# A fused attention and feed-forward kernel on one core: one written order for all five engines up to step 17, some of GpSimd's operations on VectorE, and other places for the turned queries

## The chip, the core and the metric

The kernel runs on one core of a Trainium2 chip. The core has five engines with a line of instructions each, which are taken strictly one after the other: TensorE (PE in the profile, its weight loads PEld), VectorE (DVE), ScalarE (ACT), GpSimd (POOL) and SyncE (SP), which here issues every DMA. The metric is the device time in microseconds of one execution, lower is better.

## What is computed

Per batch (8) and head (8), with 576 positions and 64 columns, queries are normalised over the columns, keys over the positions, and no attention matrix is formed. The result, laid out as 4608 tokens by 512, goes through a feed-forward block.

```python
q_s = exp(q - max(q, -1)); q_s /= sum(q_s, -1) + 1e-9
k_s = exp(k - max(k, 2));  k_s /= sum(k_s, 2) + 1e-9
kv  = einsum('bhsd,bhse->bhde', k_s, v)
x   = einsum('bhsd,bhde->bhse', q_s, kv)   # -> 4608 x 512
h   = x @ w_in                             # w_in 512 x 2048, float64
out = (h - tanh(h)) @ w_out                # w_out 2048 x 512, float64
```

## The kernel before

**Numbers.** The products are made of two float32r parts each (a rounded part and the rest), three matmuls for one: high by high, high by rest, rest by high. So every operand needs a cast (ScalarE) and a subtraction (the rest). The weights come as the two 32-bit words of a float64 and are decoded on the chip, one piece of 128 x 512 at a time, 16 pieces `i` of w_in and 16 pieces `o` of w_out: a clamp on VectorE (L118), two scalings on ScalarE (L121, L124), a shift-and-or on VectorE (L127), the cast on ScalarE (L133) and the rest on GpSimd (L134).

**Steps.** Tokens are taken in nine chunks of 512, the 2048 hidden columns in 16 pieces; a step is one pair (chunk, piece), 144 in all. The steps go 0,0 to 0,7, then all 16 of chunk 1, then 0,8 to 0,15, then chunk after chunk, so that step n is (0,n) for n below 8 and (1,n-8) for n from 8 to 23. A step has 12 matmuls `ph` (L484), then on ScalarE `u`, `t`, `vv`, `m` (L488 to L496) and the cast `gh` (L501), on VectorE `g` (L492), `t` minus (L497), `g` again (L498) and a predicated copy (L499), on GpSimd the rest `gl` (L504), and 12 matmuls `po` (L527), which PE takes two steps later. Chunk 0's first half is laid aside in DRAM (`aside`) and added later.

**Attention.** A batch needs the maximum of its keys `km` (L193 to L197), its transposition `pm` and spreading `pb`, a subtraction and exp of the keys, 40 small matmuls `pk` (L265), and the division into `kvs` (L278 to L281). Queries are reduced and subtracted (`mq` L341, GpSimd L342), exp'd, summed (`sq` L355), multiplied on GpSimd (`qn` L380), turned on PE (`pt` L395), copied (`qs` L400), multiplied with `kvs` (`px` L421), and split into `xh` (L434) and `xl` (L435), the input of `ph`. Chunk 0 needs batch 0, chunk 1 batch 1 and so on.

**What sets the order.** A first block (L591 to L645) fixes all five engines by the order of the code: batch 0, pieces i0 and i1, and the first chunk's queries. After that only PE and SP follow the code (L661); where VectorE, ScalarE and GpSimd take the steps, the decoding and batch 1's preparation is decided by a scheduler with its own idea of durations, when the program is built. Decoding is handed out at a rate of `FIRST, THEN, SPREAD` (L568), over steps 0 to 19. Batch 1's loads, all of them, stand in SP's line ahead of the pieces i4, o3 and later (`gate`, L87); the pieces i11, o10 and later stand behind the four `aside` stores.

**Places.** Pools hand out tile places by tag. `qs`, `qn` and `km` share three places (tag `qs`). `spare_q` lies in chunk 1's `xl` place, one v tile in the place of w_i15, one q tile in that of w_o15; both are late weights.

## Time and profile before

| what | value |
|---|---|
| median of 3 runs | 929.22 us (928.27 to 931.55) |
| the profiled execution | 932.16 us |
| its span, first to last instruction | 930.0 us |
| busy over the span: PE, PEld, DVE, ACT, POOL | 96%, 78%, 66%, 55%, 36% |
| first `ph` matmul of step 0 | 32.23 us |
| first `ph` matmul of step 18 (1,10) | 169.84 us |

The profile is of one execution; positions are in us from the span's start. A row of a group gives line, engine, operation, out<-in, shape and count, then after the bar its busy time, the mean ns of one, and the idle time of the engine just before with what ended it. A row of windows gives busy time (and instructions) of each engine within a stretch, then the clock granted to PE as a share and the DMA's share and rate. A row of waits gives who waited <- for what, the us in total, the times, the longest. A row of the chain gives start, length and what.

### The profile page before, as it was taken

What the parts mean: (1) busy time and instruction counts of PE and PEld (TensorE: products, weight loads), DVE (VectorE), ACT (ScalarE), POOL (GpSimd) and SP (SyncE); (2) the same over time, 40 slices, a digit from 0 to 9 for tenths busy, and PEclk for the clock granted to TensorE, in tenths of its full rate; (3) what the DMA queues carried; (4) which work ended last, traced back from release to release, by engine and by line L of the source; (5) the groups of instructions that cost most, each with busy time, mean ns of one, the idle gap of its engine ahead of it and who ended that gap; (6) DMA issues with size and microseconds to landing.
All of it is one profiled execution on the core that took longest, in us unless ns stands there. A gap on an engine that the chain in (4) does not pass through costs nothing.

```text
span 930.0 us, 13178 instructions
## 1 busy us (share of the span) xinstructions
PE 890.6 (96%) x4996; PEld 723.6 (78%) x4996; DVE 610.6 (66%) x875; ACT 555.0 (60%) x967; POOL 333.3 (36%) x277
## 2 busy tenths in 40 slices
...
GB/s 269 297 202 2 1 289 96 1 42 118 1 114 40 119 2 46 35 103 24 24 45 102 24 1 68 76 39 1 88 28 0 1 69 12 1 1 46 1 1 45
DMA packets 79775, 57.47 MB, mean 62 GB/s; under 512 B 14688, under 2 KB 72032, under 8 KB 79712
## 3 DMA queue, kind: packets, MB, share of 16 engines
...
## 4 chain that ended last, share of the span: by engine, by line
PE 75%; DVE 9%; DMA 6%; ACT 6%; issue 2%; POOL 2%; SPq 0%; DVEq 0%; ACTq 0%; POOLq 0%
PE po L527 35%; PE ph L484 34%; DMA q<-in_q_dram 3%; PE pk L265 2%; DVE g L498 2%; DMA k<-in_k_dram 2%; PE px L421 1%; PE pt L395 1%; DVE g L499 1%; DVE g L492 1%; DVE t L497 1%; ACT gh L501 1%; ACT t L490 1%; ACT u L488 1%; DMA raw_i<-in_moe_w_in_dram 1%
## 5 line engine op out<-in xcount | busy, mean ns | idle before, releaser
L527 PE MATMUL po<-w_o,gh 128*128 128x512 f32 x1152 | 361.6, 395 | 0.5 <-ACT gh L501 0.5
L504 POOL TENSOR_TENSOR gl<-g,gh 128x512 fp32r<-128x512 f32 x143 | 193.0, 1350 | 416.7 <-ACT gh L501 389.9
L484 PE MATMUL ph<-xh,w_i 128*128 128x512 f32 x1152 | 317.9, 398 | 5.0 <-ACT xh L434 3.5
L484 PEld LDWEIGHTS ph<-xh,w_i 128*128 128x128 f32 x1152 | 214.8, 190 | 52.5 <-ACT xh L434 5.0
L527 PEld LDWEIGHTS po<-w_o,gh 128*128 128x128 f32 x1152 | 215.9, 189 | 48.4 <-issue 1.4
L492 DVE SCALAR_TENSOR_TENSOR g<-u,ph 128x512 f32<-128x512 f32 x144 | 98.3, 683 | 227.6 <-ACT t L490 225.7
L527 PE MATMUL po<-w_o,gl 128*128 128x512 f32 x576 | 226.9, 394 | 9.4 <-POOL gl L504 9.4
L501 ACT CAST gh<-g 128x512 fp32r<-128x512 f32 x144 | 89.4, 621 | 193.0 <-DVE g L499 188.5
L484 PE MATMUL ph<-xl,w_i 128*128 128x512 f32 x576 | 156.3, 393 | 2.2 <-DVE xl L435 2.2
L498 DVE SCALAR_TENSOR_TENSOR g<-vv,g 128x512 f32<-128x512 f32 x144 | 124.6, 865 | 22.4 <-ACT vv L494 11.9
L527 PEld LDWEIGHTS po<-w_o,gl 128*128 128x128 f32 x576 | 109.0, 189 | 34.9 <-POOL gl L504 11.1
L488 ACT ACTIVATE u<-ph 128x512 f32<-128x512 f32 x144 | 85.8, 596 | 76.1 <-PE ph L484 75.9
L484 PEld LDWEIGHTS ph<-xl,w_i 128*128 128x128 f32 x576 | 108.5, 189 | 27.4 <-DVE xl L435 3.8
L499 DVE COPY_PREDICATED g<-m,t 128x512 f32<-128x512 int32 x144 | 120.1, 834 | 3.7
L496 ACT ACTIVATE m<-ph 128x512 int32<-128x512 f32 x144 | 86.5, 601 | 35.5 <-DVE g L492 35.2
L494 ACT ACTIVATE vv<-u,b_pa 128x512 f32<-128x512 f32 x144 | 104.8, 727 | 1.7 <-DVE g L498 1.7
L497 DVE TENSOR_TENSOR t<-ph,t 128x512 f32<-128x512 f32 x144 | 97.8, 679 | 1.9 <-ACT m L496 1.8
L490 ACT ACTIVATE t<-ph 128x512 f32<-128x512 f32 x144 | 85.3, 593 | 0.0
L342 POOL TENSOR_TENSOR q<-q,mq 128x1024 f32<-128x1024 f32 x15 | 30.1, 2009 | 61.8 <-DVE mq L341 57.0
L380 POOL TENSOR_TENSOR qn<-q,sq 128x512 f32<-128x512 f32 x30 | 32.4, 1082 | 24.2 <-PE pt L395 13.0
L341 DVE TENSOR_REDUCE mq<-q 128x16 f32<-128x1024 f32 x15 | 18.3, 1218 | 25.7 <-DMA q<-in_q_dram 25.7
L134 POOL TENSOR_TENSOR w_o<-c_o,w_o 128x512 fp32r<-128x512 f32 x16 | 25.7, 1605 | 8.4 <-ACT w_o L133 8.3
...
## 6 DMA issues: line engine op xcount, KB each, us to landing
...
out_dram<-o SPq DMA_DIRECT2D x28, 256.0 KB, 2.1
...
```

Source lines behind the costliest of these rows:

```text
L484: nc.tensor.matmul(ph, w[:, i, c], x[:, c, :], start=(n == 0), stop=(n == len(ops) - 1))
L488: nc.scalar.activation(u, ph, AF.Square)
L490: nc.scalar.activation(t, ph, AF.Tanh)
L492: nc.vector.scalar_tensor_tensor(g, u, C2, ph, op0=ALU.mult, op1=ALU.mult)
L494: nc.scalar.activation(vv, u, AF.Square, bias=b_pa)
L496: last = nc.scalar.activation(m, ph, AF.Square, scale=M_SCALE)
L497: nc.vector.tensor_tensor(t, ph, t, op=ALU.subtract)
L498: nc.vector.scalar_tensor_tensor(g, vv, PB, g, op0=ALU.add, op1=ALU.mult)
L499: nc.vector.copy_predicated(g, m, t)
L501: nc.scalar.copy(gh, g)
L504: eng.tensor_tensor(gl, g, gh.bitcast(F32), op=ALU.subtract)
L527: nc.tensor.matmul(po[t], g[:, cols], wt["o", f][:, w], start=(begin and n == 0), stop=(end and n == 2),)
```

## The change

A string `ORDER` of 576 names lists every small operation of the first 17 steps (n from 0 to 16, their `po` up to step 14), of batches 0 and 1, of chunk 0's and 1's first 512 tokens' queries, of the loads and of the decoding of all 32 pieces. Each operation that was a part of a longer function has become a function of its own, and the list calls them one by one, inside a block that fixes all five engines. Two lines of it:

```python
u0 st.i4 k1.2 t0 ld.i6 vv0 g0 m0 tt0 ca.i4 gg0 ph2 v1.0 u1 sub.i4 t1 g1 vv1 tt1 lo.o2 ld.i7 gg1
pr.o2 cp0 u2 st.o2 pr.o1 k1.1 cl.i6 gh0 st.o1 m1 gl0* t2 ph3 q3 cp1 ca.o2 ca.o1 cl.i5 sub.o2*
```

`ld` is a load, `cl pr lo st ca sub` the decoding, `u t vv m g tt gg cp gh gl` a step. A star puts an operation on VectorE that else is GpSimd's: 31 names have one, 15 `sub`, 13 `gl`, 2 `qn` and 1 `qu` (the query subtraction). From step 17 on the code is as before, but no piece is left to decode; the scheduler still places the other three engines' instructions of later steps, and some of batch 2 come among the listed ones. The core of the diff:

```diff
-        with tc.issue_after(gate[-1].ins) if gate else nullcontext():
-            ...
-            nc.gpsimd.tensor_tensor(w[:, 1], cf, w[:, 0].bitcast(F32), op=ALU.subtract)
+        def rest(eng):
+            w = wt[kind, f]
+            eng.tensor_tensor(
+                w[:, 1], st["c"].bitcast(F32), w[:, 0].bitcast(F32), op=ALU.subtract
+            )
+        return dict(cl=clamp, pr=scale, lo=low, st=shift, ca=cast, sub=rest)
...
+    def q_keep(i: int):
+        unit, j = tiles[i]
+        late = {(0, 0): f"wo{NF - 3}", (1, 0): f"wo{NF - 2}", (1, 1): f"wi{NF - 2}"}
+        if unit in late and unit not in spare:
+            spare[unit] = wts.tile([P, 2, NC, P], F32, name=f"spare_qs{i}", tag=late[unit])
+        if unit in spare:
+            qs = spare[unit][:, j]
+        else:
+            qs = ap.tile([P, NC, P], F32, name=f"qs{i}", tag="qs", bufs=3)
+        nc.scalar.copy(qs, qs_of[i])
...
+        def gl(eng):
+            eng.tensor_tensor(
+                new("gl", F32R), st["g"], st["gh"].bitcast(F32), op=ALU.subtract
+            )
...
-    FIRST, THEN, SPREAD = 4, 2 * F0 + 1, 12
+    PLANNED, SPREAD = 17, 3
...
     with tc.manual_schedule(engines={ENG.PE, ENG.DVE, ENG.Activation, ENG.Pool, ENG.SP}):
-        kv_load(0, st)
-        ...
+        for name in ORDER.split():
+            eng = (nc.vector,) if name[-1] == "*" else ()
+            ...
+            ops[name](*eng)
+            done.add(name)
...
-        for n, (j, f) in enumerate(steps):
+        for n, (j, f) in enumerate(steps[PLANNED:], PLANNED):
```

The turned queries of the tiles (0,0), (1,0) and (1,1) so lie in the places of w_o13, w_o14 and w_i14 until `px` has read them; those three pieces can be loaded only after that.

**PE, from step 0 on.** `ph0_1` is `ph` of chunk 0, piece 1; `po0_0_2` is the sum of chunk 0 that was opened at piece 0, token tile 2, and the `w_o` beside it tells the piece; the last number of a name is the tile's own. Before:

```order
L220 MATMUL pb1_507<-ident_r_84,ml1_454 128x128
L265 MATMUL pk1_522<-v1_0_428,k1_0_422 64x65 x16
L484 MATMUL ph0_2_539<-xh0_285,w_i2_367 128x512 x4
L484 MATMUL ph0_2_539<-xl0_286,w_i2_367 128x512 x4
L484 MATMUL ph0_2_539<-xh0_285,w_i2_367 128x512 x4
L527 MATMUL po0_0_0_587<-w_o0_357,gh0_0_398 128x512 x2
L527 MATMUL po0_0_0_587<-w_o0_357,gl0_0_400 128x512
L527 MATMUL po0_0_1_591<-w_o0_357,gh0_0_398 128x512 x2
```

Now:

```order
L544 MATMUL ph0_1_433<-xh0_365,w_i1_373 128x512 x4
L544 MATMUL ph0_1_433<-xl0_366,w_i1_373 128x512 x4
L544 MATMUL ph0_1_433<-xh0_365,w_i1_373 128x512 x4
L544 MATMUL ph0_2_467<-xh0_365,w_i2_391 128x512 x4
L544 MATMUL ph0_2_467<-xl0_366,w_i2_391 128x512 x4
L544 MATMUL ph0_2_467<-xh0_365,w_i2_391 128x512 x4
L544 MATMUL ph0_3_517<-xh0_365,w_i3_429 128x512 x4
L544 MATMUL ph0_3_517<-xl0_366,w_i3_429 128x512 x4
L544 MATMUL ph0_3_517<-xh0_365,w_i3_429 128x512 x4
L635 MATMUL po0_0_0_550<-w_o0_423,gh0_0_507 128x512 x2
L635 MATMUL po0_0_0_550<-w_o0_423,gl0_0_513 128x512
```

Before, batch 1's `pm`, `pb` and `pk` stand among the first steps, with `ph` of step 2 and `po` of step 0 behind them. Now four `ph` stand in a row ahead of `po` of step 0, and batch 1's `pm` comes after `po` of step 3. Not shown: at the end of the list `ph` of step 17 now stands ahead of `po` of step 14, before it stood behind.

**VectorE, around the split of chunk 0's second half** (`xl0<-px2`). Before:

```order
L435 TENSOR_TENSOR xl0_286<-px0_0_287,xh0_285 128x2x256
L435 TENSOR_TENSOR xl0_286<-px0_1_288,xh0_285 128x2x256
L193 TENSOR_TENSOR km1_434<-k1_0_422 128x512
L127 SCALAR_TENSOR_TENSOR c_i1_266<-raw_i1_124 128x512
L196 TENSOR_TENSOR km1_434<-km1_434,k1_1_424 128x512 x2
L197 TENSOR_TENSOR km1_434<-km1_434,kr1_426 64x512
L435 TENSOR_TENSOR xl0_286<-px2_0_329,xh0_285 128x2x256
L435 TENSOR_TENSOR xl0_286<-px2_1_330,xh0_285 128x2x256
L118 TENSOR_SCALAR raw_o0_126<-raw_o0_126 128x512
L118 TENSOR_SCALAR raw_i2_128<-raw_i2_128 128x512
L341 TENSOR_REDUCE mq1_0_579<-q1_0_442 128x16
```

Now the same split, and then the first place where batch 1's `km` comes:

```order
L145 TENSOR_SCALAR raw_o2_275<-raw_o2_275 128x512
L486 TENSOR_TENSOR xl0_366<-px2_1_321,xh0_365 128x2x256
L486 TENSOR_TENSOR xl0_366<-px2_0_320,xh0_365 128x2x256
L167 TENSOR_TENSOR w_i1_373<-c_i1_363,w_i1_373 128x512
L486 TENSOR_TENSOR xl0_366<-px0_1_346,xh0_365 128x2x256
L486 TENSOR_TENSOR xl0_366<-px0_0_345,xh0_365 128x2x256
```

```order
L565 SCALAR_TENSOR_TENSOR g0_2_542<-u0_2_499,ph0_2_467 128x512
L570 TENSOR_TENSOR t0_2_515<-ph0_2_467,t0_2_515 128x512
L584 TENSOR_TENSOR gl0_1_568<-g0_1_488,gh0_1_539 128x512
L223 TENSOR_TENSOR km1_575<-k1_0_414 128x512
L573 SCALAR_TENSOR_TENSOR g0_2_542<-vv0_2_570,g0_2_542 128x512
L226 TENSOR_TENSOR km1_575<-km1_575,k1_1_504 128x512
L578 COPY_PREDICATED g0_2_542<-mk0_2_548,t0_2_515 128x512
```

Before, four operations on batch 1's keys stand ahead of the second pair of `xl`, and the reduction of batch 1's queries soon behind. Now the pairs of `xl` stand together with a `sub` of piece i1 (w_i) between them, and batch 1's `km` stands behind steps 0 and 1, with step 1's `gl`, formerly GpSimd's, just ahead of it.

**SP and VectorE, where chunk 0's first half is laid aside and batch 2 begins.** SP before:

```order
L89 DMA raw_i10_1053<-in_moe_w_in_dram 128x4x128
L94 DMA raw_o9_1105<-in_moe_w_out_dram 128x512
L551 DMA aside_100<-aside0_1118 128x512 x2
L551 DMA aside_100<-aside2_1129 128x512 x2
L89 DMA raw_i11_1167<-in_moe_w_in_dram 128x4x128
L94 DMA raw_o10_1223<-in_moe_w_out_dram 128x512
L89 DMA raw_i12_1275<-in_moe_w_in_dram 128x4x128
```

SP now:

```order
L123 DMA raw_i15_945<-in_moe_w_in_dram 128x4x128
L123 DMA raw_i14_1034<-in_moe_w_in_dram 128x4x128
L128 DMA raw_o14_1077<-in_moe_w_out_dram 128x512
L733 DMA aside_100<-aside1_1110 128x512
L733 DMA aside_100<-aside3_1152 128x512 x2
L189 DMA k2_0_1700<-in_k_dram 128x8x128
L733 DMA aside_100<-aside1_1110 128x512
L189 DMA k2_1_1702<-in_k_dram 128x8x128
L194 DMA kr2_1704<-in_k_dram 64x8x64
```

VectorE now:

```order
L584 TENSOR_TENSOR gl1_0_1183<-g1_0_1147,gh1_0_1178 128x512
L156 SCALAR_TENSOR_TENSOR c_o8_1188<-raw_o8_696 128x512
L565 SCALAR_TENSOR_TENSOR g1_1_1196<-u1_1_1185,ph1_1_1128 128x512
L570 TENSOR_TENSOR t1_2_1194<-ph1_2_1160,t1_2_1194 128x512
L573 SCALAR_TENSOR_TENSOR g1_1_1196<-vv1_1_1198,g1_1_1196 128x512
L223 TENSOR_TENSOR km2_1742<-k2_0_1700 128x512
L565 SCALAR_TENSOR_TENSOR g1_2_1223<-u1_2_1205,ph1_2_1160 128x512
L578 COPY_PREDICATED g1_1_1196<-mk1_1_1181,t1_1_1173 128x512
```

The loads of the late pieces no longer stand behind the `aside` stores; batch 2's first key tile stands behind three of them and the second behind the fourth (both take the places of the `aside` tiles). On VectorE the scheduler has set the first operation on batch 2's keys between those of steps 9 and 10.

More of the change, by code (lines that the diff above doesn't have):

```diff
@@ L1 @@
-from contextlib import ExitStack, contextmanager, nullcontext
+from contextlib import ExitStack
 import numpy as np
@@ L80, in attn_moe_kernel @@
     staged = {}
-    gate = []
     wt = {}
@@ L506, in h_step @@
+    def h_step(j: int, f: int):
+        parts = h_parts(j, f)
+        last = None
+        eng = nc.vector if (j, f) == (NCH - 1, NF - 1) else nc.gpsimd
+        for name, part in parts.items():
+            if name == "last":
+                last = part()
+            elif name == "gl":
+                part(eng)
+            else:
+                part()
         return last
@@ new lines, in o_mm @@
+        if begin:
+            po[t] = ps_o.tile([P, DM], F32, name=f"po{j}_{f}_{t}", tag="o")
+        cols = slice(t * P, (t + 1) * P)
+        for n, (g, w) in enumerate(((gh, 0), (gh, 1), (gl, 0))):
+            nc.tensor.matmul(
+                po[t],
+                g[:, cols],
+                wt["o", f][:, w],
+                start=(begin and n == 0),
+                stop=(end and n == 2),
+            )
+        if (j, f) == (0, F0 - 1):
+            spare["po", t] = po[t]
+        return end
@@ new lines, in o_aside, with o_out @@
+    def o_aside(t: int):
+        pair = "aside", t // 2
+        if pair not in spare:
+            spare[pair] = ap.tile([P, 2, DM], F32, name=f"aside{t}", tag="k", bufs=NKP)
+        spare["aside of", t] = o = spare[pair][:, t % 2]
+        nc.scalar.copy(o, spare["po", t])
+    def o_out(j: int, f: int, t: int):
+        if j == 0:
+            o = back[t // 2][:, t % 2]
+            nc.vector.tensor_tensor(o, po[t], o, op=ALU.add)
+        elif j == NCH - 1 and t % 2:
+            o = gp.tile([P, DM], F32, name=f"o{j}_{f}_{t}", tag="g")
+            nc.vector.tensor_copy(o, po[t])
+        else:
+            o = dec.tile([P, DM], F32, name=f"o{j}_{f}_{t}", tag="c")
+            nc.scalar.copy(o, po[t])
+        for rows, p0, p1 in rows_of(out, j * TPC + t):
+            nc.sync.dma_start(rows, o[p0:p1])
@@ new lines, in attn_moe_kernel @@
+    for kind, f in pieces:
+        ops[f"ld.{kind}{f}"] = lambda kind=kind, f=f: load_weight(kind, f)
+        for part, fn in split_weight(kind, f).items():
+            ops[f"{part}.{kind}{f}"] = fn
+    for n, (j, f) in enumerate(steps[:PLANNED]):
+        for part, fn in h_parts(j, f).items():
+            ops[f"{part}{n}"] = fn
+        for t in range(TPC):
+            ops[f"po{n}.{t}"] = lambda j=j, f=f, t=t: o_mm(j, f, t)
+    for t in range(TPC):
+        ops[f"ev.{t}"] = lambda t=t: o_aside(t)
+        ops[f"sv.{t}"] = lambda t=t: nc.sync.dma_start(aside[t], spare["aside of", t])
@@ L590, in attn_moe_kernel @@
     ENG = mybir.EngineType
+    done = set()
     with tc.manual_schedule(engines={ENG.PE, ENG.DVE, ENG.Activation, ENG.Pool, ENG.SP}):
-        kv_load(0, st)
-        q_load(q0)
-        q_load(q1)
-        load_weight(*pieces[0])
-        v_load(0, st, 0)
-        v_load(0, st, 1)
-        v_load(0, st, 2)
-        for n in range(1, 4):
-            load_weight(*pieces[n])
-        loaded = 4
-        decode = [split_weight(*pieces[n]) for n in range(2)]
-        def go(*ns):
-            for n in ns:
-                next(decode[n])
```

523 lines of the change are left out of this document (271 added, 252 removed).

## The prediction

> **What bounds the kernel now.** I read the page first, then the busy time by stages, then PE's waits, then the operations of VectorE one kind at a time, then the timeline at the places where PE stood.
>
> ```profile
> span 930.0 us, 13178 instructions
> PE 890.6 (96%) x4996; PEld 723.6 (78%) x4996; DVE 610.6 (66%) x875; ACT 555.0 (60%) x967; POOL 333.3 (36%) x277
> ```
>
> Over the whole span PE is busy 96%, which says little about its ends. The windows by stage, cut at 23.1 (the end of batch 0's division), 32.2 (first `ph`), 73.3 (`ph` of step 3), 142.8 and 169.8 (`ph` of step 18):
>
> ```profile
> 0.00:23.10 23.10, 17.37 (x156) 16.07 (x156) 15.00 (x24) 6.72 (x8) 8.50 (x22) 0.85 1.02 269
> 32.20:73.30 41.10, 25.38 (x140) 19.08 (x140) 34.09 (x51) 24.33 (x40) 22.45 (x13) 0.68 0.67 220
> 73.30:142.80 69.50, 68.57 (x361) 54.67 (x357) 52.41 (x77) 59.64 (x112) 37.22 (x30) 1.00 0.33 112
> 142.80:169.80 27.00, 21.84 (x85) 16.59 (x85) 24.21 (x32) 20.76 (x39) 17.10 (x13) 0.94 0.31 45
> 169.80:930.00 760.20, 751.56 (x4189) 612.84 (x4188) 479.04 (x685) 437.36 (x760) 245.06 (x201) 1.00 0.15 40
> ```
>
> Behind 169.8 PE idles 8.6 of 760 us at full clock: nothing can be gained there by the order of the first 17 steps, and I let that part move as a block. Between 73.3 and 142.8 PE idles 0.9. The loss lies in the second row, where PE idles 15.7 us at a clock of 0.68 while DVE is busy 34.1 of 41.1, and in the fourth, where PE idles 5.2 and DVE 2.8 of 27.0. The pace of PE when nothing holds it, from the chain:
>
> ```profile
> 167.28 2.72 PE po L527 x12
> 170.00 2.72 PE ph L484 x12
> ```
>
> The first `ph` of step 0 and of step 18 in the timeline:
>
> ```profile
> 32.23 2.08 PE L484 MATMUL ph<-xh,w_i 128*128 128x512 f32 x4 [0.83 <-ACT xh L434]
> 169.84 1.07 PE L484 MATMUL ph<-xh,w_i 128*128 128x512 f32 x4
> ```
>
> Up to `ph` of step 18 PE has 18 `ph` and 16 `po`: 34 x 2.72 = 92.5 us, and I put batch 1's small matmuls at 7.5 (an estimate: the stage 73.3 to 142.8 holds 23 groups, 62.6 of its 69.5 us, so four turnings and two `px` took about 6 with the idle time; `pm`, `pb`, `pk` come on top). That is 100; from 32.2 on it took 137.6. So 37 us is what a perfect order could bring with the first `ph` where it is. Who held PE, up to 169.8:
>
> ```profile
> PE po L527 <- POOL gl L504: 8.9, 3, 5.2
> PE pb L220 <- DVE mh L209: 6.6, 2, 5.0
> PE pk L265 <- ACT k L253: 3.1, 1, 3.1
> PE ph L484 <- DVE xl L435: 2.2, 2, 1.4
> ```
>
> Three are VectorE's line or GpSimd's `gl`; the third is an exp that itself waited for VectorE's subtraction. The timeline shows how a load holds what has nothing to do with it:
>
> ```profile
> 31.90 2.42 DVE L196 TENSOR_TENSOR km<-km,k 128x512 f32<-128x512 f32 x2 [0.86 <-DMA k<-in_k_dram]
> 34.96 1.27 DVE L435 TENSOR_TENSOR xl<-px,xh 128x512 fp32r<-128x512 f32 x2
> 39.14 1.22 DVE L341 TENSOR_REDUCE mq<-q 128x16 f32<-128x1024 f32 x1 [2.23 <-DMA q<-in_q_dram]
> ```
>
> `xl`, without which step 0 can't go on, stands behind batch 1's keys; step 0's own `g` comes after batch 1's queries. So up to step 17 the bound is VectorE: its work, its place in line, and what GpSimd does to it.
>
> **The change part by part.** I count VectorE's time up to the end of step 15's `gl`, the last thing that `po` of step 15 waits for. Before, the same content stands done at 165.2 (17 `g` to predicated copy, 27 shifts, 32 clamps):
>
> ```profile
> 0.00:165.20 165.20, 134.43 (x788) 106.97 (x789) 129.34 (x188) 113.59 (x201) 84.84 (x74) 0.87 0.56 163
> ```
>
> *What it has to do.* Groups within 0 to 165, mean ns of one behind the busy time:
>
> ```profile
> L504 POOL TENSOR_TENSOR gl<-g,gh 128x512 fp32r<-128x512 f32 x16 | 24.5, 1536 | 27.1 <-ACT gh L501 23.8 <-PE px L421 3.3
> L134 POOL TENSOR_TENSOR w_o<-c_o,w_o 128x512 fp32r<-128x512 f32 x13 | 21.8, 1676 | 8.2 <-ACT w_o L133 8.2
> L498 DVE SCALAR_TENSOR_TENSOR g<-vv,g 128x512 f32<-128x512 f32 x17 | 19.0, 1117 | 3.4 <-ACT vv L494 2.8
> L497 DVE TENSOR_TENSOR t<-ph,t 128x512 f32<-128x512 f32 x17 | 11.5, 678 | 0.1
> L118 DVE TENSOR_SCALAR raw_o<-raw_o 128x512 f32<-128x512 f32 x16 | 11.9, 741 | 0.9 <-DMA raw_o<-in_moe_w_out_dram 0.9
> L118 DVE TENSOR_SCALAR raw_i<-raw_i 128x512 f32<-128x512 f32 x16 | 10.3, 646 | 2.3 <-DMA raw_i<-in_moe_w_in_dram 2.3
> L127 DVE SCALAR_TENSOR_TENSOR c_i<-raw_i 128x512 uint32<-128x512 uint32 x14 | 10.8, 771 | 0.2
> L196 DVE TENSOR_TENSOR km<-km,k 128x512 f32<-128x512 f32 x6 | 6.7, 1124 | 2.5 <-DMA k<-in_k_dram 2.4
> ```
>
> `t` (L497), which reads `ph`, takes 0.68; the second `g` (L498), of the same shape and with both inputs in SBUF, 1.12. The clamp alone takes 0.42 and one beside GpSimd's work 1.5:
>
> ```profile
> 36.49 0.42 DVE L118 TENSOR_SCALAR raw_i<-raw_i 128x512 f32<-128x512 f32 x1
> 142.79 1.46 POOL L504 TENSOR_TENSOR gl<-g,gh 128x512 fp32r<-128x512 f32 x1
> 143.04 1.76 DVE L498 SCALAR_TENSOR_TENSOR g<-vv,g 128x512 f32<-128x512 f32 x1
> 144.73 1.51 DVE L118 TENSOR_SCALAR raw_o<-raw_o 128x512 f32<-128x512 f32 x1
> ```
>
> The stretched operations end as GpSimd's do. Taking 0.68 (clamp 0.42) as undisturbed, the stretching cost 17 x 0.44 + 16 x 0.32 + 16 x 0.23 + 27 x 0.09 + 6 x 0.45 = 21 us. So VectorE's bare work was 129.3 - 21 = 108. The stars add, up to that point, 13 `gl`, 13 `sub` and 2 `qn`, of 128 x 512, and one `qu` of twice the size. How long `gl` takes on VectorE one instruction shows (the last step's), and two `xl` in 1.27 above show that the second in a row adds 0.6:
>
> ```profile
> L504 DVE TENSOR_TENSOR gl<-g,gh 128x512 fp32r<-128x512 f32 x1 | 0.7, 692 | 0.8 <-ACT gh L501 0.8
> ```
>
> 28 x 0.6 + 1.2 = 18: bare work 126 us, of which nothing lies beside other VectorE work. GpSimd loses 26 x 1.5 + 4.5 = 44 of its 85 us, about 41 remain. Stretching goes with GpSimd's time and with the instructions exposed: 21 x 41/85 x 114/85 = 13.5 (85 exposed before: the second `g`, clamps, shifts, `km`; 29 more now). Ends: 0 and GpSimd's whole 41. I take 11, a little under the scaling, since a chain from `g` to `gl` that stays on VectorE meets GpSimd less.
>
> The Trainium skill ("SBUF — State Buffer", "Who interferes with whom") states that VectorE with two SBUF inputs and GpSimd reading SBUF exclude each other for a whole instruction, and "Perfetto Trace Analysis" ("Optimizing Scalar/DVE Operations") that moving work between the two might not help for that reason. The rows above agree on the exclusion; by that rule the 11 would be anything up to 41, which is the second rival. The rows also show the other side: 1.5 us of GpSimd's time is given for 0.6 of VectorE's.
>
> *Where it stands idle.* Before, 165.2 - 129.3 = 36 us:
>
> ```profile
> DVE g L492 <- ACT t L490: 11.9, 10, 1.9
> DVE km L193 <- DMA k<-in_k_dram: 5.0, 1, 5.0
> DVE sl L278 <- PE pk L265: 4.8, 1, 4.8
> ```
>
> The first key tile is still the first thing needed, and batch 0's `pk` still stands ahead of its division: 9.8 us stay. The 11.9 of `g` behind `t` come from one step's chain after another; the list puts other steps' and pieces' work between, I leave 2 of them (between 0 and 6). The waits for loads of batch 1 (2.4 and 2.2 in the rows above) go, since weights come first and batch 1's keys stand behind step 1. What comes in their place: the scheduler has set the first operation on batch 2's keys behind step 9's second `g`, and that tile's DMA stands behind three `aside` stores:
>
> ```profile
> 273.19 5.42 DMA k<-in_k_dram
> ```
>
> That is a key tile's landing later on, in the chain; and the stores, by the table of DMA issues, with the median us to landing last:
>
> ```profile
> aside<-aside SPq DMA_DIRECT2D x4, 256.0 KB, 2.1
> ```
>
> From the copy that frees the last of them: 2.1 to be stored, about 0.5 to be issued, 5.4 to land, 8 in all, against some 4 us of VectorE's work in between. That is 4 us of standing, and behind it queue step 10's `g` and all else; the second key tile, behind the fourth store, some 3 more. I take 6 (0 to 8). Idle: 9.8 + 2 + 6 = 18.
>
> *The sum.* 126 + 11 + 18 = 155 for the end of step 15's `gl`; `po` of step 15 takes 2.7 more, so `ph` of step 18 begins at 157.5 to 158 instead of 169.84. The gain is 12 us. PE's floor, 29 + 100 = 129 (first `ph` some 3 us earlier, as `xl` no longer waits for `km`), and ScalarE's, 114 of work before and no more now, both lie under it. The other edits come to nothing: splitting functions adds no instruction; eleven of the warming matmuls now stand right ahead of step 0, 2 to 4 us by the row below (two records for one, 28 before), where PE waits about 3 us for `xh` and `xl` anyhow; the queries in w_o13's place are read by batch 0's `px`, those in the places of w_i14 and w_o14 by batch 1's, and these two are the last weights that SP loads, for steps 21 and 22; the decoding ends earlier or later by a few us but is needed only from step 17 on.
>
> ```profile
> L148 PE MATMUL warm<-ident 128*128 128x128 f32 x56 | 11.3, 387 | 1.4 <-POOL ident masks.py:199 1.4
> ```
>
> The profiled execution: span 930 - 12 = 918, 2.2 outside it, 920.2. The median of the runs lies 2.9 below the profiled execution's 932.16; so the forecast is 917 us.
>
> **The rivals.** A difference of 0.3% (2.8 us) is about what a measurement of this kernel can tell from none.
>
> *PE becomes the bound.* If VectorE and GpSimd hardly meet (3 instead of 11) and batch 2's keys are not waited for, VectorE ends at 126 + 3 + 11 = 140, `ph` of step 18 begins at 143, 27 us earlier: 902 us. For it: the chain `g` to `gl` stays on one engine for 13 of 16 steps, and PE's 8.9 us of waiting for `gl` go. Against it: 30 of the 61 listed operations stay on GpSimd, each as long as before. Chance 0.2.
>
> *Slower: VectorE is held by GpSimd.* Now nearly every operation of VectorE that GpSimd could hold stands in a line that all steps go through. If each of GpSimd's 41 us is waited for three times in four, the stretching is 31 instead of 11, the end 175, step 18 at 178: 8 us later, 937 us. It decides from a stretching of 23 us, where the gain is gone. For it: before, VectorE lost 21 with three quarters of the exposed instructions. Against it: GpSimd has half the work. Chance 0.11.
>
> *No change: VectorE waits for DMAs.* The list fixes where each clamp stands. Batch 2's two key tiles, loaded among late weights before, took over 12 us each to land, not 5.4:
>
> ```profile
> DMA to landing us min/median/max: 11.8/12.5/13.3
> ```
>
> If that holds again, or the clamps of the first pieces find their loads as late as the waits of 2.3 and 0.9 us above, 8 to 12 us of the gain go: 925 to 929 us. Half of it is still faster. Against it: the late weights now load earlier. Chance 0.16.
>
> The forecast itself, 907 to 924 us, has 0.53.
>
> **How the numbers follow.** Faster: 0.53 + 0.2 + half of 0.16, 0.81. Within 0.3%: 0.09. Slower: 0.1. The range from 899 to 930 takes in the first rival but its far end and most of the third, and leaves out the second.
>
> **What would show each step.** VectorE's busy time up to step 15's `gl` near 137; the second `g`'s mean in 0 to 150 down from 1117 toward 900; GpSimd near 40 in the same stretch; PE's idle between the first `ph` and step 3 under 8 us; a wait of the first operation on batch 2's keys for its DMA of some 4 us; `ph` of step 18 near 158, and from there the same time to the end as before (760). I am wrong if step 18 begins earlier than 148 or after 168, or if the part behind it changes by more than 2 us.

## The result, and the profile after

The changed kernel takes 919.47 us (median of 4 runs, 918.5 to 920.62) against 929.02 us before (4 runs, 928.27 to 931.55): ratio 0.9893, 95% interval 0.9869 to 0.9917. The forecast was 917.0 with a range of 899 to 930. In the experiments below one run of e6_fast took 4096.7 us and one of the kernel before, in the last comparison, 1002.57; the ratios leave these two out, the medians do not. The profiled execution took 920.28 us, its span is 918.5. The head of its page:

```profile
span 918.5 us, 13209 instructions
PE 890.2 (97%) x5034; PEld 721.9 (79%) x5034; DVE 615.4 (67%) x906; ACT 556.1 (61%) x967; POOL 288.2 (31%) x246
```

As before, the shares over the span say little about the ends. The line numbers have moved: `ph` is L544, `po` L635, the step's ScalarE work L559, `g` L565 and L573, `gl` L584, a piece's rest `sub` L167. The timeline at the first `ph` of step 0 and of step 18:

```profile
30.52 0.74 PE L544 MATMUL ph<-xh,w_i 128*128 128x512 f32 x2
...
154.01 1.07 PE L544 MATMUL ph<-xh,w_i 128*128 128x512 f32 x4
```

Step 18 begins 15.8 us earlier than before (169.84), while the span is only 11.5 shorter. So 4.3 us were lost again behind it, in a part whose instructions stand in the same order on PE as before. The windows up to the end of step 15's `gl` (151.2 now), from the first `ph` to step 3, and behind step 18:

```profile
0.00:151.20 151.20, 132.24 (x836) 106.75 (x836) 130.91 (x215) 118.48 (x209) 40.98 (x45) 0.94 0.60 178
30.50:45.40 14.90, 10.68 (x39) 7.70 (x37) 13.39 (x21) 12.69 (x24) 2.64 (x3) 0.89 1.11 296
154.00:918.50 764.50, 755.49 (x4189) 613.17 (x4187) 481.79 (x690) 436.05 (x756) 245.94 (x200) 1.00 0.15 40
```

Third column of numbers behind the stretch's length: DVE is busy 130.9 of the first 151.2 (129.3 of 165.2 before), so it stands idle 20.3 instead of 36; POOL, two columns on, is down from 84.8 to 41.0. PE idles 4.2 us between the first `ph` and step 3, where it idled 15.7; but PE's order has changed, and these stretches hold 39 matmuls now and 140 before. The fairer count goes from the first `ph` to step 18, where the work is nearly the same (the changed kernel's row stands beside e10_pe's below):

```profile
32.23:169.84 137.61, 115.82 (x581) 90.35 (x581) 110.72 (x159) 104.74 (x189) 76.78 (x54) 0.89 0.43 131
```

There PE idled 21.8 us and idles 12.1 now. Of the 15.8 us, 9.7 are idle time, 4.4 are shorter busy time (115.8 to 111.4 us, at a granted clock of 0.96 instead of 0.89), and 1.7 come from the earlier first `ph`. In the last of the three rows above PE does the same 4189 instructions as before in 755.5 us of busy time instead of 751.6: the loss behind step 18 is busy time of PE, not waiting. The groups of VectorE up to 152 us, mean ns of one behind the busy time:

```profile
L573 DVE SCALAR_TENSOR_TENSOR g<-vv,g 128x512 f32<-128x512 f32 x17 | 15.3, 899 | 1.7 <-ACT vv L559 1.6
L584 DVE TENSOR_TENSOR gl<-g,gh 128x512 fp32r<-128x512 f32 x13 | 8.9, 688 | 0.2 <-ACT gh L581 0.2
L145 DVE TENSOR_SCALAR raw_o<-raw_o 128x512 f32<-128x512 f32 x16 | 8.5, 538 | 0.0
L145 DVE TENSOR_SCALAR raw_i<-raw_i 128x512 f32<-128x512 f32 x15 | 6.7, 455 | 0.0
L167 DVE TENSOR_TENSOR w_i<-c_i,w_i 128x512 fp32r<-128x512 f32 x6 | 5.9, 986 | 0.3 <-ACT w_i L163 0.3
L226 DVE TENSOR_TENSOR km<-km,k 128x512 f32<-128x512 f32 x6 | 5.1, 851 | 2.2 <-DMA k<-in_k_dram 2.2
```

The second `g` is down from 1117 to 899 ns, the clamps from 741 and 646 to 538 and 455: less of VectorE's time goes to standing beside GpSimd (e4_allstar below, where GpSimd does next to nothing, has 685, 423 and 426 ns). The waits of PE up to 154 us and of VectorE up to 152, and VectorE's two operations that wait for batch 2's keys:

```profile
PE ph L544 <- ACT mk L559: 6.0, 3, 2.2
PE pm L235 <- DVE km L229: 4.8, 1, 4.8
PE ph L544 <- DVE t L570: 2.0, 1, 2.0
PE po L635 <- DVE gl L584: 1.5, 2, 1.3
...
DVE km L223 <- DMA k<-in_k_dram: 6.2, 2, 5.1
DVE g L573 <- ACT vv L559: 1.6, 1, 1.6
DVE g L565 <- ACT mk L559: 1.4, 2, 0.7
DVE t L570 <- ACT mk L559: 1.3, 2, 0.7
```

```profile
110.30 0.69 DVE L223 TENSOR_TENSOR km<-k 128x512 f32<-128x512 f32 x1 [1.08 <-DMA k<-in_k_dram]
...
121.55 0.69 DVE L226 TENSOR_TENSOR km<-km,k 128x512 f32<-128x512 f32 x1 [0.98 <-DMA k<-in_k_dram]
```

`po` behind GpSimd's `gl` (8.9 us before) is gone, and PE's largest wait now is `ph` for ScalarE's `mk`, which reads one of the two banks that `ph` alternates between. (`pm` for `km`, 4.8, is batch 0's, ahead of the first `ph`.) The waits for batch 2's keys are 2.1 us in all.

### The profile page after: what moved, and what is told of

It reads as the page before. It is cut to its first block, busy times and chain, and to the rows that moved or that the text cites. A ratio compares the mean times of both kernels' runs of the same rounds, so it can differ in the third digit from the quotient of the medians.

```text
span 918.5 us, 13209 instructions
## 1 busy us (share of the span) xinstructions
PE 890.2 (97%) x5034; PEld 721.9 (79%) x5034; DVE 615.4 (67%) x906; ACT 556.1 (61%) x967; POOL 288.2 (31%) x246
## 4 chain that ended last, share of the span: by engine, by line
PE 77%; DVE 7%; ACT 5%; DMA 4%; issue 4%; POOL 2%; SPq 0%; DVEq 0%; ACTq 0%; POOLq 0%
PE po L635 37%; PE ph L544 35%; PE pk L299 2%; DMA k<-in_k_dram 2%; PE px L465 1%; PE pt L437 1%; DVE g L573 1%; DVE g L565 1%; DVE g L578 1%; DMA spare_q<-in_q_dram 1%; ACT gh L581 1%; DVE t L570 1%; DMA raw_o<-in_moe_w_out_dram 1%; POOL d L267 1%; DMA q<-in_q_dram 1%
## 5 line engine op out<-in xcount | busy, mean ns | idle before, releaser
L635 PE MATMUL po<-w_o,gh 128*128 128x512 f32 x1152 | 361.5, 395 | 1.5 <-DVE w_o L167 1.5
L544 PE MATMUL ph<-xh,w_i 128*128 128x512 f32 x1152 | 317.7, 398 | 10.3 <-ACT mk L559 6.0
L584 POOL TENSOR_TENSOR gl<-g,gh 128x512 fp32r<-128x512 f32 x130 | 172.6, 1328 | 389.7 <-ACT gh L581 373.5
L544 PEld LDWEIGHTS ph<-xh,w_i 128*128 128x128 f32 x1152 | 214.6, 190 | 59.3 <-ACT mk L559 7.3
L635 PEld LDWEIGHTS po<-w_o,gh 128*128 128x128 f32 x1152 | 214.7, 188 | 51.0 <-DVE w_o L167 1.8
L565 DVE SCALAR_TENSOR_TENSOR g<-u,ph 128x512 f32<-128x512 f32 x144 | 98.3, 682 | 219.2 <-ACT t L559 202.2
L635 PE MATMUL po<-w_o,gl 128*128 128x512 f32 x576 | 226.4, 393 | 1.5 <-DVE gl L584 1.5
L544 PE MATMUL ph<-xl,w_i 128*128 128x512 f32 x576 | 157.9, 397 | 0.0
L559 ACT ACTIVATE u<-ph 128x512 f32<-128x512 f32 x144 | 85.8, 596 | 81.4 <-PE ph L544 81.1
L573 DVE SCALAR_TENSOR_TENSOR g<-vv,g 128x512 f32<-128x512 f32 x144 | 120.4, 836 | 20.0 <-ACT vv L559 10.4
L544 PEld LDWEIGHTS ph<-xl,w_i 128*128 128x128 f32 x576 | 109.8, 191 | 25.0 <-DVE xl L486 0.6
L635 PEld LDWEIGHTS po<-w_o,gl 128*128 128x128 f32 x576 | 108.1, 188 | 27.0 <-DVE gl L584 2.4
L578 DVE COPY_PREDICATED g<-mk,t 128x512 f32<-128x512 int32 x144 | 118.8, 825 | 3.3
L559 ACT ACTIVATE vv<-u,b_pa 128x512 f32<-128x512 f32 x144 | 104.5, 726 | 6.9 <-DVE g L573 6.8
L559 ACT ACTIVATE mk<-ph 128x512 int32<-128x512 f32 x144 | 86.2, 599 | 35.9 <-DVE g L565 32.3
L559 ACT ACTIVATE t<-ph 128x512 f32<-128x512 f32 x144 | 85.2, 592 | 1.1 <-PE ph L544 1.1
L389 POOL TENSOR_TENSOR q<-q,mq 128x1024 f32<-128x1024 f32 x14 | 27.7, 1979 | 47.5 <-DVE mq L384 44.6
L423 POOL TENSOR_TENSOR qn<-q,sq 128x512 f32<-128x512 f32 x28 | 31.9, 1142 | 28.1 <-DVE sq L403 14.6
L167 POOL TENSOR_TENSOR w_i<-c_i,w_i 128x512 fp32r<-128x512 f32 x10 | 14.5, 1451 | 52.2 <-ACT w_i L163 42.6
```

What stands on the lines that cost most here:

```text
L389: eng.tensor_tensor(qf, qf, mq, op=ALU.subtract)
L423: eng.tensor_tensor(qn.rearrange("p a g d -> p g a d"), qt[:, :, j].rearrange("p (g a) d -> p g a d", g=2), sq[:, :, j : j + 1] .broadcast ...
L544: nc.tensor.matmul(ph, w[:, i, c], x[:, c, :], start=(n == 0), stop=(n == len(ops) - 1))
L559: st["last"] = nc.scalar.activation(new(tag, **of), st[src], fn, **kw)
L565: nc.vector.scalar_tensor_tensor(new("g"), st["u"], C2, st["ph"], op0=ALU.mult, op1=ALU.mult)
L573: nc.vector.scalar_tensor_tensor(st["g"], st["vv"], PB, st["g"], op0=ALU.add, op1=ALU.mult)
```

## The experiments

Each time is a median; the kernel before, run beside each group of them on the same chip, took 930.07 us in the first eight comparisons and 930.09 in the last four. A step's first `ph` is given as "step 18 at ...", read from the timeline of that run; "behind" is the rest of its span. Both come from one profile each. The changed kernel and six of the runs (e1, e3, e4, e8, e9, e10) have all their weights in the same places; "behind" goes from 761.4 to 764.6 among them, and PE's busy time there from 754.7 to 755.8. So a difference under some 3 us in that column tells little, while one of 2 us in the busy time does.

| run | edit | us | ratio to before, 95% | step 18 at | behind |
|---|---|---|---|---|---|
| e1_nostar | changed, no star | 922.92 | 0.9921 (0.9900 to 0.9941) | 156.9 | 764.6 |
| e2_stars_only | before, with the 31 stars | 925.30 | 0.9953 (0.9934 to 0.9972) | 164.4 | 759.3 |
| e3_sched | list binds PE and SP only, from step 0 | 954.54 | 1.0248 (1.0219 to 1.0277) | 191.8 | 761.4 |
| e4_allstar | changed, all 61 on VectorE | 919.54 | 0.9883 (0.9866 to 0.9900) | 155.6 | 761.8 |
| e6_fast | changed, weights 64 bytes on | 913.70 | 0.9823 (0.9799 to 0.9847) | 151.7 | 757.9 |
| e7_slow | changed, no weight 64 bytes on | 924.54 | 0.9939 (0.9920 to 0.9957) | 153.0 | 770.0 |
| e8_act | changed, 17 more casts on ScalarE | 924.37 | 0.9936 (0.9919 to 0.9953) | 159.2 | 762.5 |
| e9_dve | changed, 17 more casts on VectorE | 922.83 | 0.9922 (0.9903 to 0.9941) | 156.7 | 763.1 |
| e10_pe | changed, 51 more matmuls on PE | 919.23 | 0.9890 (0.9873 to 0.9907) | 152.7 | 764.5 |
| e12_fast_ca | e6, five casts on GpSimd | 911.76 | 0.9805 (0.9788 to 0.9822) | 153.5 | 756.7 |
| e13_fast_allstar | e6, all 61 on VectorE | 914.34 | 0.9839 (0.9820 to 0.9857) | 156.8 | 755.5 |
| e14_before_fast | before, weights 64 bytes on | 928.30 | 0.9980 (0.9969 to 0.9991) | 168.6 | 757.6 |

### The order and the stars apart

The list without its stars (all 61 on GpSimd):

```diff
-            eng = (nc.vector,) if name[-1] == "*" else ()
+            eng = ()
```

> The written order as changed, but every starred operation stays on GpSimd (as before the change). Theory A (the order counts: it takes idle time out of VectorE's line; the stars cost VectorE 18 us of work and give 11 us of stretching back): VectorE has 7 us less to do up to step 15's gl, GpSimd 44 us more; the time stays within 5 us of the changed kernel's 919.5, say 915 to 925. Theory B (the stars count: gl and sub come sooner and VectorE is stretched less): the gain is gone, 927 us or more, with PE waiting over 8 us for gl on GpSimd.

And the kernel before with the same 31 operations on VectorE; PE's and SP's order stays, and the scheduler places the other three engines anew:

```diff
+STAR_SUB = "i1 o0 i3 o2 i5 o4 o5 o7 i9 o8 i10 o12 i14 o13 o10".split()
+STAR_GL = [(0, n) if n < 8 else (1, n - 8) for n in (0, 1, 2, 4, 6, 7, 8, 9, 10, 12, 13, 14, 15)]
-        eng = nc.vector if (j, f) == (NCH - 1, NF - 1) else nc.gpsimd
+        eng = nc.vector if (j, f) == (NCH - 1, NF - 1) or (j, f) in STAR_GL else nc.gpsimd
...
```

> The kernel before, with its own order and places, but the same 31 operations on VectorE (the other three engines' order is the scheduler's, made anew). Theory A: VectorE was already the late one and gets 18 us more, its idle time stays; 927 to 935 us. Theory B: most of the gain, 919 to 922 us, and PE's 8.9 us of waiting for GpSimd's gl gone.

The order without stars, its new places for the weights included, is worth 7.2 us (930.07 to 922.92), the stars alone, in the old order of PE and SP, 4.8. Both together bring 9.6, so the stars bring 2 to 3.5 more where the order is there already. Each of the two parts gains by itself. The window up to step 18 in e1_nostar, and its waits of PE for GpSimd:

```profile
0.00:156.90 156.90, 134.43 (x846) 108.04 (x847) 133.41 (x189) 119.84 (x210) 80.62 (x74) 0.96 0.57 171
```

```profile
PE po L635 <- POOL w_o L167: 2.6, 2, 2.0
...
PE po L635 <- POOL gl L584: 1.8, 3, 0.7
```

The changed kernel up to its own step 18:

```profile
0.00:154.00 154.00, 134.66 (x846) 108.73 (x847) 133.60 (x218) 120.01 (x211) 42.27 (x46) 0.94 0.59 175
```

This shows that stars cost VectorE very little. Up to the same point of PE's order it does 29 operations more with them (218 against 189), 17 us at some 0.6 us each, and yet is busy only 0.2 us longer (133.6 against 133.4), while GpSimd does 38.4 us less. What VectorE did not do itself, it had paid for by longer operations beside GpSimd's. Two of its groups in e1_nostar show which, up to 152 us:

```profile
L578 DVE COPY_PREDICATED g<-mk,t 128x512 f32<-128x512 int32 x16 | 15.7, 980 | 0.9 <-ACT mk L559 0.9
L145 DVE TENSOR_SCALAR raw_i<-raw_i 128x512 f32<-128x512 f32 x15 | 14.9, 1006 | 0.0
```

With the stars the predicated copies take 794 ns and these clamps 455, which gives back 8.3 us on the clamps alone. The second `g` is not among them: it takes 894 ns without stars and 899 with them, so its fall from 1117 came with the order.

In e2_stars_only PE waits elsewhere: the largest wait up to step 18 is one exp of the keys in batch 1's line, which the list puts between other work.

```profile
PE pk L268 <- ACT k L256: 7.2, 1, 7.2
```

### Whose order it is

The list binds all five engines ahead of the first `ph`; behind it only PE and SP, as in the kernel before, and the scheduler places the other three:

```diff
-    with tc.manual_schedule(engines={ENG.PE, ENG.DVE, ENG.Activation, ENG.Pool, ENG.SP}):
-        for name in ORDER.split():
+    names = ORDER.split()
+    first = names.index("ph0")
+    for part, engines in (
+        (names[:first], {ENG.PE, ENG.DVE, ENG.Activation, ENG.Pool, ENG.SP}),
+        (names[first:], {ENG.PE, ENG.SP}),
+    ):
```

> The changed kernel, whose list fixes all five engines only up to step 0; behind that the list fixes PE and SP alone, and the scheduler places VectorE, ScalarE and GpSimd (the stars stay). Theory A: the order of the three engines is what gains, so more than half of it goes: 924 us or more. Rival (the order of PE and of the loads is enough, since weights and batch 1's parts come in another sequence): 918 to 921 us.

```profile
PE ph L544 <- DVE t L570: 12.1, 1, 12.1
PE po L635 <- DVE gl L584: 7.2, 3, 3.9
```

954.5 us, 24 more than before and 35 more than with the list on all five. PE's order is the same, and it now waits 12.1 us at one place for VectorE's `t`. So PE's and SP's order does not gain by itself: it needs VectorE, ScalarE and GpSimd in the order for which it was made. The converse, these three in the list's order with PE and SP as before, was not run.

### VectorE alone, or more engines

All 61 operations on VectorE, none on GpSimd:

```diff
-            eng = (nc.vector,) if name[-1] == "*" else ()
+            eng = (nc.vector,) if name[-1] == "*" or name.rstrip("0123456789") in ("qu", "qn", "gl") or name[:3] == "sub" else ()
```

> The changed kernel with all 61 such operations of the list on VectorE, none on GpSimd. Theory A (VectorE bounds): 30 more operations, about 20 us of work, less some 10 us of stretching that goes: step 18 begins 8 to 10 us later, 926 to 930 us. Theory B (GpSimd's hold on VectorE is what costs): 914 to 919 us. Theory C (ScalarE, 92% busy between 60 and 112 us, is the bound by now): within 2 us of 919.5.

919.54 us, the same as with 31. The row up to step 18:

```profile
0.00:155.60 155.60, 132.77 (x847) 106.80 (x848) 140.14 (x245) 120.73 (x213) 3.25 (x19) 0.97 0.59 173
```

VectorE is busy 6.5 us more than in the changed kernel (27 operations more) and step 18 begins 1.6 us later, not 6: the theory that VectorE alone sets the pace all the way fell here. Two of its groups, and its stage from step 4 to step 8:

```profile
L573 DVE SCALAR_TENSOR_TENSOR g<-vv,g 128x512 f32<-128x512 f32 x17 | 11.6, 685 | 1.0 <-ACT vv L559 0.9
L145 DVE TENSOR_SCALAR raw_o<-raw_o 128x512 f32<-128x512 f32 x16 | 6.7, 423 | 0.0
49.20:98.20 49.00, 42.16 (x303) 32.72 (x302) 47.48 (x84) 43.85 (x78) 0.34 (x2) 0.97 0.52 180
```

With GpSimd out of the way nothing of the stretching is left in these groups. But the 1.6 us are a sum: step 4 begins 3.4 us earlier than in the changed kernel, its stage to step 8 is 5.8 us longer (49.0 against 43.2, VectorE idle for 1.5), and the rest 0.8 shorter. So the other 30 operations are not free for VectorE in that stage. To see who sets the pace, the same amount of work was added to one engine at a time, in the 17 listed steps; nothing reads its result. On ScalarE, and then on VectorE (`nc.vector.tensor_copy` in the same place):

```diff
+    scr = const.tile([P, CH], mybir.dt.bfloat16, name="scr")
             nc.scalar.copy(new("gh", F32R), st["g"])
+            if (j, f) in steps[:PLANNED]:
+                nc.scalar.copy(scr, st["g"])
```

> The changed kernel with one extra cast of g into a scratch tile on ScalarE in each of the 17 listed steps, behind gh (17 x 0.62 = 10.5 us of added ScalarE work; nothing reads it). Theory V (VectorE alone sets the pace up to step 17, ScalarE has 33 us of slack by 151 us): +0 to +3 us, 919 to 922.5. Theory S (ScalarE sets the pace too between 60 and 112 us, where it is 92% busy): +5 to +10, 924.5 to 930. Theory W (each is bound by its chain of waits, neither engine): +0 to +3 here and for the same work on VectorE.

> The changed kernel with the same extra cast on VectorE instead (17 casts, between 0.46 and 0.69 us each by the rows of similar operations, so 8 to 12 us of added VectorE work, in the order right behind gh's place). Theory V: +8 to +12 us, 927.5 to 931.5. Theory S (two engines near the bound, each hiding some): +4 to +8, 923.5 to 927.5. Theory W: +0 to +3.

And on PE:

```diff
+        if (j, f) in steps[:PLANNED]:
+            for n in range(3):
+                nc.tensor.matmul(ph, w[:, 0, 0], xh[:, 0, :], start=True, stop=True)
```

> The changed kernel with three more matmuls at the head of each of the 17 listed steps, into the same bank that the step's own first matmul then overwrites (51 x 0.227 us = 11.6 us of added TensorE work; nothing reads it). TensorE stood idle for 12.1 us between 30.5 and 154.0 us by the windows (4.2 + 4.9 + 3.0). Theory A (VectorE and ScalarE set the pace by turns, TensorE waits for them): most of the work goes into that idle time, +0 to +3 us, 919.5 to 922.5. Theory B (three engines all near their bound, as the two runs with added ScalarE and VectorE work at 0.4 to 0.5 us per us suggest): +4 to +7, 923.5 to 926.5. Theory C (the rival on record that TensorE becomes the bound): +9 to +12, 928.5 to 931.5.

17 casts of 0.615 us on ScalarE (10.5 us) cost 4.9 us. 17 on VectorE of 0.45 us in the mean (7.6 us) cost 3.4. The 11.6 us on PE cost nothing: 919.23 against 919.47. So PE does not set the pace up to step 18, and neither of the other two does so alone. Where each is shows when the stretch is cut at step 4 and step 8. The windows from step 4 to step 8 and from step 8 to step 18, of the changed kernel:

```profile
52.60:95.80 43.20, 39.77 (x303) 31.61 (x302) 42.19 (x72) 41.65 (x75) 14.33 (x12) 1.00 0.64 217
95.80:154.00 58.20, 53.77 (x220) 41.70 (x219) 52.09 (x82) 44.83 (x81) 12.91 (x9) 0.97 0.24 60
```

of e8_act:

```profile
52.90:100.80 47.90, 42.85 (x303) 33.66 (x301) 42.54 (x71) 44.31 (x80) 13.66 (x12) 0.93 0.57 194
100.80:159.20 58.40, 52.62 (x220) 40.57 (x220) 52.37 (x83) 49.88 (x92) 12.91 (x9) 1.00 0.22 60
```

and of e9_dve:

```profile
52.00:96.30 44.30, 41.82 (x302) 32.81 (x302) 42.45 (x78) 42.02 (x75) 15.67 (x12) 0.96 0.63 215
96.30:156.70 60.40, 54.04 (x221) 41.64 (x220) 54.72 (x91) 45.38 (x82) 13.80 (x9) 0.97 0.22 58
```

In the changed kernel's first row VectorE is idle for 1.0 us of 43.2 and ScalarE for 1.6: both are full. Work added to ScalarE (2.7 us more busy) makes this stage 4.7 us longer, more than was added, and VectorE then stands idle for 5.4: waits of one for the other come on top, which were not followed one by one. The work added to VectorE, 6 operations, costs 1.1 there. In the second row VectorE is idle for 6.1 of 58.2 and ScalarE for 13.4: there the added ScalarE work (5.0 us more busy) costs 0.2, and the added VectorE work (2.6 more busy) 2.2. So, as far as single profiles show it, ScalarE and VectorE bound steps 4 to 8 together, and VectorE more than ScalarE steps 8 to 17.

The row of e10_pe from the first `ph` to 154 us, the same of the changed kernel, and e10_pe from step 8 to step 18:

```profile
30.50:154.00 123.50, 117.86 (x639) 94.24 (x638) 114.41 (x186) 105.51 (x190) 31.23 (x27) 1.00 0.49 147
```

```profile
30.50:154.00 123.50, 111.42 (x582) 86.72 (x581) 113.22 (x183) 104.87 (x188) 31.45 (x27) 0.96 0.50 148
```

```profile
94.80:152.70 57.90, 57.02 (x247) 46.03 (x246) 52.16 (x83) 44.16 (x82) 11.59 (x8) 1.00 0.23 59
```

Half of the idle time is filled (5.6 us of 12.1 are left), and the time does not move. PE is busy only 6.4 us more in the first row, though 11.6 were added; the granted clock is 1.00 there and 0.96 in the changed kernel, so this addition is not as clean as the other two. And the room is used up: from step 8 to step 18 PE is busy 57.0 of 57.9 us.

### The part behind step 18: where the weights start

Behind step 18 PE has 126 `ph` and 128 `po` of 12 matmuls. The mean distance from one `po` matmul to the next, taken from their starts in steps 40 to 139 for each of w_out's 16 pieces apart (distances over 300 ns, with other matmuls or a wait between, left out), has two values: about 226.7 ns and about 233. Before, pieces 0, 1 and 2 were at 233, now 0 to 5, 13 and 15 are (pieces 6 and 12, where other matmuls stand between, are at 231 and 230 in both). The built program lists where each tile starts. A pool gives its tags their places in the order of their first use, and one place in the pool of weights is 64 bytes longer than the rest, since a tile of values waits in it (`spare_v1`, in w_i15's). Weights placed ahead of it start at 96 bytes behind a multiple of 128, those behind it at 32. The list's loads come in another order, and the turned queries' tiles take their places early: w_o3, w_o4, w_o5, w_o13 and w_o15 went from 32 to 96. Two kernels move the long place, with no instruction moved on any engine. First in the pool:

```diff
+    H2 = 2 * D + 2
+    wts.tile([P, H, H2], F32, name="first", tag=f"wi{NF - 1}")
```

> The changed kernel with one line that makes the tag of w_in's last piece the first to get a place in the pool of weights; its place is 64 bytes longer than the others (it also holds a tile of values), so that every other weight lies 64 bytes further on and starts at 32 behind a multiple of 128 where eleven of them did so before; the order of the instructions is the same on every engine. Theory L (a second-layer matmul's spacing follows from where the moved-in weight starts: 226.7 ns at 32 behind a multiple of 128, about 233 ns at 96, as read from the traces of both kernels): the spacing of pieces 0 to 5, 13 and 15 falls from about 233 to about 227 ns, 8 pieces x 12 matmuls x 6.3 ns x 7.3 passes = 4.4 us of TensorE work goes behind step 18 (755.5 toward 751.1 us busy), and the time is 914 to 916.5 us. Rival R (the spacing comes from the order, or from the change of buffers, and the place is chance): 918.5 to 920.5, spacings as in the changed kernel.

Last in the pool (all other tags are touched ahead of it):

```diff
+    for f in range(NF):
+        for kind in "io":
+            if (kind, f) != ("i", NF - 1):
+                wts.tile([P, DM], I64, name=f"first_{kind}{f}", tag=f"w{kind}{f}")
```

> The changed kernel with the long tag given its place last, so that every weight starts at 96 behind a multiple of 128; same order of instructions. Theory L: pieces 7 to 11 and 14 slow down to 233 ns as well, 6 x 12 x 6.3 ns x 7.3 = 3.3 us more TensorE work behind step 18, time 921.5 to 924. Rival R: 918.5 to 920.5.

| | before | after | e6_fast | e7_slow |
|---|---|---|---|---|
| w_out pieces at 96 | 3 | 8 | 0 | 16 |
| w_in pieces at 96 | 5 | 9 | 1 | 16 |
| `po` spacing, mean of the 16 pieces, ns | 228.4 | 230.5 | 227.3 | 233.1 |
| `ph` spacing, mean of the 16 pieces, ns | 229.0 | 229.4 | 228.0 | 230.8 |
| time, us | 929.0 to 930.1 | 919.47 | 913.70 | 924.54 |

A single step shows it in the chain. Start, length and what, of the changed kernel:

```profile
349.59 2.80 PE po L635 x12
352.39 0.44 PE pm L235 x4
352.83 2.77 PE ph L544 x12
355.60 2.79 PE po L635 x12
```

and the same steps in e6_fast:

```profile
346.18 2.72 PE po L637 x12
348.90 0.44 PE pm L237 x4
349.34 2.77 PE ph L546 x12
352.11 2.72 PE po L637 x12
```

Twelve matmuls take 2.72 us from the one place and 2.80 from the other. The windows behind step 18 of e6_fast and of e7_slow:

```profile
151.70:909.60 757.90, 748.82 (x4189) 612.83 (x4187) 483.04 (x690) 436.09 (x756) 245.12 (x200) 1.00 0.15 40
```

```profile
153.00:923.00 770.00, 761.81 (x4189) 613.33 (x4187) 480.80 (x690) 436.18 (x756) 246.97 (x200) 1.00 0.14 40
```

The same 4189 instructions keep PE busy for 748.8, 755.5 or 761.8 us, by where the weights start alone. The expected sizes (4.4 and 3.3 us) were too small, since they counted w_out only: `ph`, which has w_in's pieces as its loaded weights and not as the moved-in operand, goes from 229.4 to 228.0 and 230.8 ns as well. With it (230.5 - 227.3) x 1536 + (229.4 - 228.0) x 1512 matmuls = 7.0 us, beside 6.7 measured. From before to after the same sum is 2.1 x 1536 + 0.4 x 1512 = 3.8, beside 3.9 us of busy time: the loss behind step 18 is this one. The same line in the kernel before, where it moves three pieces of w_out and four of w_in:

> The kernel before with the same single line for the places, so that its four slow pieces of the second layer's and first layer's weights lie 64 bytes further on; order of instructions as before on every engine. Theory L (place): 3 x 12 x 6.3 ns x 7.3 passes = 1.7 us less from w_out's pieces 0, 1 and 2 behind step 18, some tenths more ahead of it and from w_in: ratio 0.9965 to 0.9985, 926 to 928.5 us. If the place matters only in the changed kernel's order: ratio 1.000, 929 to 931.

The ratio is 0.9980 (0.9969 to 0.9991): the place works in the old order too. With the places equal (e14_before_fast and e6_fast) the part behind step 18 takes 757.6 and 757.9 us, and nothing of the 4.3 us is left. Then the change takes the time from 928.30 to 913.70 us, 14.6 us instead of 9.6.

### On from the better places

> Weights 64 bytes further on, and all 61 listed operations on VectorE, none on GpSimd. If place and engine act apart from each other: 919.5 - 5.8 = 913.7, so 912.5 to 915, the same as with half of them on GpSimd. If the faster TensorE makes VectorE's work the longer (VectorE 136 us of the first 151): 916 to 920.

914.34 us against e6_fast's 913.70: place and engine act apart from each other, since all 61 on VectorE made no difference at the old places either (919.54 against 919.47).

Five of ScalarE's casts of weight pieces given to GpSimd, on top of e6_fast:

```diff
-            nc.scalar.copy(w[:, 0], st["c"].bitcast(F32))
+            if (kind, f) in (("o", 3), ("i", 6), ("i", 7), ("o", 6), ("i", 8)):
+                nc.gpsimd.tensor_copy(w[:, 0], st["c"].bitcast(F32))
+            else:
+                nc.scalar.copy(w[:, 0], st["c"].bitcast(F32))
```

> The kernel of the run with the weights 64 bytes further on (913.7 us), and five of ScalarE's casts of weight pieces (o3, i6, i7, o6, i8, those whose subtraction is GpSimd's already) given to GpSimd: 5 x 0.62 = 3.1 us less on ScalarE between 52 and 100 us. If ScalarE sets the pace there (the added casts cost 0.5 us per us): 1 to 3 us less, 910.7 to 912.7. If VectorE or GpSimd pays instead (a longer hold of GpSimd beside VectorE's operations, casts that come late for their subtraction): 913.5 to 917.

GpSimd's groups up to 160 us in this run, where a cast takes 1.5 to 2.0 us against ScalarE's 0.62:

```profile
L166 POOL CAST w_i<-c_i 128x512 fp32r<-128x512 f32 x3 | 4.4, 1483 | 12.1 <-DVE c_i L158 12.1
L166 POOL CAST w_o<-c_o 128x512 fp32r<-128x512 f32 x2 | 4.0, 2018 | 7.1 <-DMA raw_o<-in_moe_w_out_dram 5.0 <-DVE c_o L158 2.1
```

911.76 us is the lowest median of all, but its interval (0.9788 to 0.9822) overlaps that of e6_fast (0.9799 to 0.9847; five of its six runs go from 911.4 to 917.3), and in the profiled executions step 18 begins later with it (153.5 against 151.7). So whether taking 3 us off ScalarE helps is not settled. Both versions beat the changed kernel.

## Why the prediction was right, and where it failed

**The sign and the place of the gain: right.** The loss lay between the first `ph` and step 18, in VectorE's line and in what GpSimd did to it, and the list and the stars take it out there. PE's idle time from the first `ph` to step 3 was to be under 8 us, it is 4.2 (a weak sign, since the stretch now holds 39 matmuls instead of 140; to step 18 it fell from 21.8 to 12.1). GpSimd was to be busy 41 us, it is 41.0. The second `g` was to go from 1117 toward 900 ns, it is at 899, though by the order and not by the stars (894 in e1_nostar).

**The sum up to step 15's `gl`: 155 expected, 151.2 measured.** Its terms: the stretching 11, against about 9 by the groups above (17 x 0.22 for the second `g` over its undisturbed 0.68, 16 x 0.12 + 15 x 0.04 for the clamps, 6 x 0.3 for w_i's rests, 6 x 0.17 for `km`); other groups, not counted here, are stretched a little too. VectorE's busy time 137, against 130.9, so some 4 us of the bare 126 were not there either; why stays open. Idle 18, against 20.3, from other parts than forecast. The 4.8 us behind batch 0's `pk`, which were to stay, are gone (0.1 us is left ahead of `sl`). The wait for batch 2's keys was put at 6 and is 2.1: the tiles were there sooner than 8 us behind the copy that frees their place, or VectorE had more to do until then than the 4 us taken; which of the two was not separated. What took the room are short waits, for ScalarE above all (`vv` 1.6, `mk` 1.4 and 1.3 and smaller ones, some 7.5 in all), of which the sum had 2. So step 18 began at 154.0 instead of 157.5 to 158, and the gain there was 15.8 instead of 12.

**"I let that part move as a block": this failed.** The prediction named a change of more than 2 us behind step 18 as what would make it wrong, and it is 4.3. The reason given, that PE idles there for only 8.6 us and nothing can be gained, is true of gains alone. A part that PE fills to 99% takes every nanosecond by which a matmul gets longer, and the change did touch it: the order of the loads and the new tiles for the turned queries decide where the weights start. "The other edits come to nothing" was said of instructions and of times at which a place is free, not of where the place is. The two misses, 3.8 us early and 4.3 us late, stand against each other, so 917 came within 2.5 us of 919.47 by more luck than the terms had earned. What is left of the miss is mostly the 2.9 us taken off for the profiled execution, which is only 0.8 above the median this time.

**"The bound is VectorE": half right.** For steps 8 to 17 the added work shows it, in single profiles. For steps 4 to 8 ScalarE is as full, by 41.65 of 43.2 us. The prediction compared ScalarE's 114 us with a stretch of 155 and took the rest for slack; over that one stage there is none. A cut at step 4 and step 8 would have shown what the average over stages hid.

**The rivals.** PE does not become the bound: 11.6 us more of its work cost nothing, though they left it hardly any room in steps 8 to 17. VectorE is not held longer by GpSimd: with all 61 operations on GpSimd the list still gains 7.2 us, and with 31 of them on VectorE more, not less. Of the waits for DMAs that the third rival named, VectorE's line has 2.1 us for batch 2's keys and none for a load of a piece. The Trainium skill ("Perfetto Trace Analysis", "Optimizing Scalar/DVE Operations") says that moving work between GpSimd and VectorE might not help, as they share a read port. These runs agree with the sharing: most of VectorE's operations are shorter where GpSimd does less. As to the doubt, it depends on the operations: moving the 31 made VectorE busy for 0.2 us more and gained 2 to 3.5 us, and moving the other 30 made no difference to the time that can be measured.

**Not tried.** The turned queries' new places were not taken out by themselves, since the order as it is written needs them; only what the places of the weights cost was. Why ScalarE and VectorE each give back about half of the work added to them over the whole stretch was read from two cuts of it, and not followed instruction by instruction.
